# Attention and expert layer on one core: a head's five output tiles in one PSUM bank, normalised from PSUM

## The chip, the cores and the metric

The kernel runs on one core of one Trainium2 chip. The metric is device microseconds from start to end of one execution; lower is better. The engines are PE (TensorE: matmuls, with its weight loads shown as PEld), DVE (VectorE), ACT (ScalarE), POOL (GpSimd) and SP, which issues most transfers. Each engine works through a queue of its own in order. PSUM, into which PE writes its results, has eight banks of 512 float32 per partition; DVE and ACT can read it.

## The reference

An attention over 4 batches of 8 heads (1152 keys, 576 pooled queries, head size 64), followed by a mixture of 8 experts of which each token takes one.

```python
q_pool = q.reshape(B, H, S // 2, 2, D).mean(axis=3)
scores = scale * np.matmul(q_pool, k.transpose(0, 1, 3, 2))
scores = scores - np.max(scores, axis=-1, keepdims=True)
attn = np.exp(scores)
attn = attn / (np.sum(attn, axis=-1, keepdims=True) + 1e-09)
x = np.matmul(attn, v)          # heads side by side: 2304 tokens x 512
# expert layer: argmax of a cosine router, softmax gate,
# out = gate * (relu(x @ w1[e]) @ w2[e]) for the chosen expert e
```

## The kernel before

Every float32 operand of a matmul is split into a 16-bit high part and a 16-bit rest, and products are sums of two or three matmuls. The attention stage is a loop over 32 heads `g` (two heads are a pair `p`; 16 pairs). Each head has nine slots `c`, one for each chunk of 128 keys, and in each slot the code issues, in the order `ORDER = 'SMEPLX'`:

- **S** (`sc`, L274): the scores of chunk `c` for 512 of the 576 queries, two matmuls of 512 columns into a bank of `ps_s` (L268); ACT takes the exponential (L278) into `E32`.
- **M** (`mx_half`, L212): maxima for the head that comes next. Approximate row maxima come from single matmuls, without the smallest of the split products (L224, L231), written to a tile `m` of `ps_m`, which has two banks; DVE reduces the tile to one number a row (L239). Five tiles in a pair, listed in `MXA`, go another way: ACT copies the tile to a 16-bit tile `my` (L235) and DVE reduces the copy (L237), put off by `mpend` to the next slot.
- **E** (`lo_part`, L270): the rest of the exponentials, `E32` minus its high half, on POOL or DVE by the lists `POOL_EL` and `POOL_LO` (L272).
- **P** (`pv`, L329): output tiles of the head before. Four tiles of 128 queries and a fifth of 64 (the last queries). For each of nine chunks a pair of matmuls: high part by `[V high, ones, V low]`, 129 columns (L363), and rest by `[V high, ones]`, 65 columns (L364). Each tile has a bank of `ps_p` (two banks), and ACT copies it to `AC` in SBUF when it is done (L366).
- **L** (`sl`, L283): scores of the last 64 queries, 64 columns a chunk (L268, tile `lt`), in two groups with their exponentials (L292).
- **X**: side work. Among it `mx_send` (L248), which turns the maxima round with matmuls into a tile `mt` and has ACT write them as a row of the next head's queries, loads and splits for later pairs, and in slot 5 (`NPOS = 5`, the sixth) `norm(g - 2)`.

`norm` (L368) works on `AC`, on DVE alone: add a small constant to the row sums (L378), add the two halves of the output (L379), reciprocal (L380), multiply four tiles (L382) and the fifth (L384) into `XX`. From head 9 on, steps of the router run in between, with logits in banks of `ps_p`. PSUM is full: three banks `ps_s`, two `ps_m`, one `ps_l`, two `ps_p`.

After the loop the last head is normalised in two parts, the router finishes and the expert blocks run; their weights, loaded by SP and split by ACT, DVE and POOL, take the rest of the time. The order of every engine's queue is the order in which this code is written; the tile framework only adds the waits.

Of the kernel before, what the change touches and what calls it, by code (L numbers as in the profile page):

```python
# [42 lines left out]
def attn_moe(ctx: ExitStack, tc: tile.TileContext, qt, kt, vt, emb, tau, w1, w2, out):  # L43
# [35 lines left out]
    AC = [const.tile([128, 5, 130], F32, name=f"ac{i}") for i in range(2)]  # L79
# [34 lines left out]
    st2 = LD[:, 4:8, 0:2 * DM].rearrange("p s (c f) -> p s c f", c=2)  # L114

# [89 lines left out]
    mpend = []  # L205
    work_step = [0]

    def mx_flush(lag=0):
        while mpend and mpend[0][0] + lag <= work_step[0]:
            mpend.pop(0)[1]()  # L210

    def mx_half(g, t, j):  # L212
        p, h = divmod(g, 2)
        b = p // NP
        s = p % NB2
        if (p, h) not in mc:
            mc[p, h] = work.tile([128, 3, 5], F32, tag="mc", name="mc")
        m = ps_m.tile([128, 512], F32, tag="m", name="m")
        k0 = 512 * j
        w = 512 if j < 2 else S - 1024  # L220
        ts = t if j == 2 else (t,)
        for i, u in enumerate(ts):
            if u == 4:
                nc.tensor.matmul(out=m[:, i * w:(i + 1) * w], lhsT=BD[s], rhs=hn_t[p][0][:, 0, k0:k0 + w], start=True, stop=True)  # L224
            elif p < MXN:
                c = t0(b, u)
                k, q = hn_t[p]
                nc.tensor.matmul(out=m[:, i * w:(i + 1) * w], lhsT=q[64 * h:64 * h + 64, 0, c:c + 128], rhs=k[64 * h:64 * h + 64, 0, k0:k0 + w], start=True, stop=True)
            else:
                c = t0(b, u)  # L230
                nc.tensor.matmul(out=m[:, i * w:(i + 1) * w], lhsT=QQ[s][:, h, 0, c:c + 128], rhs=KK[s][:, h, 0, k0:k0 + w], start=True, stop=True)  # L231
        n = len(ts)
        if n == 1 and [ts[0], j] in (MXA[h] if g else MXAP):
            y = work.tile([128, 512], BF16, tag="my", name="my")[:, 0:w]
            nc.scalar.activation(out=y, in_=m[:, 0:w], func=AF.Copy)  # L235
            o = mc[p, h][:, j, ts[0]:ts[0] + 1]
            mpend.append((work_step[0], lambda: nc.vector.tensor_scalar(out=y, in0=y, scalar1=-3e38, scalar2=None, op0=ALU.max, op1=ALU.max, accum_out=o)))  # L237
            return
        nc.vector.tensor_reduce(out=mc[p, h][:, j, ts[0]:ts[0] + n], in_=m[:, 0:n * w].rearrange("p (t k) -> p t k", t=n), axis=AX.X, op=ALU.max)  # L239

    def mx_row(g, lo=0, hi_=5):
        p, h = divmod(g, 2)
        n = min(hi_, 5 if h == 0 else 4)
        m = mc[p, h]
        mx_flush()
        nc.vector.tensor_reduce(out=MH[g % 2][:, 64 + lo:64 + n], in_=m[:, :, lo:n].rearrange("p j t -> p t j"), axis=AX.X, op=ALU.max)

    def mx_send(g, main=True, left=True):  # L248
        p, h = divmod(g, 2)
        b = p // NP  # L250
        s = p % NB2
        c = t0(b, 0)
        if main:
            t = ps_p.tile([128, 512], F32, tag="p", name="mt")
            for i in range(4):
                nc.tensor.matmul(out=t[0:65, 128 * i:128 * i + 128], lhsT=MH[g % 2][:, i:i + 65], rhs=ident, start=True, stop=True)
            nc.scalar.activation(out=QQ[s][64:65, h, 1, c:c + 512], in_=t[64:65], func=AF.Copy, scale=-1.0, bias=ESL)
        if h == 0 and left:
            l0 = lo0(b)
            t = ps_p.tile([128, 512], F32, tag="p", name="mt")  # L260
            nc.tensor.matmul(out=t[0:65, 0:128], lhsT=MH[g % 2][:, 4:69], rhs=ident, start=True, stop=True)
            nc.scalar.activation(out=QQ[s][64:65, :, 1, l0:l0 + 64], in_=t[64:65, 0:128].rearrange("o (h q) -> o h q", h=2), func=AF.Copy, scale=-1.0, bias=ESL)
# [52 lines left out]
    MPOS = [0, 0, 0]  # L315
    NPOS = 5
# [14 lines left out]
    MXN = 2  # L331
# [18 lines left out]

    def pv(g, t, c0_, c1_):
        p, h = divmod(g, 2)
        b, i = divmod(p, NP)
        s = p % NB2
        if t < 4:
            c0, n, o = t0(b, t), 128, 0
        else:
            c0, n, o = lo0(b), 64, 64 * (b % 2)
        if c0_ == 0:
            acc[0] = ps_p.tile([128, 512], F32, tag="p", name="acc")  # L360
        a = acc[0]
# [115 lines left out]
    def front(b, c1, now=False):  # L477
# [8 lines left out]
        def logit(i, L=None):  # L486
# [3 lines left out]
            L = ps_p.tile([128, 512], F32, tag="p", name="L")  # L490
# [32 lines left out]
    def chains(b, last=None):  # L523
# [14 lines left out]
        def rank():  # L538
            L = ps_p.tile([128, 512], F32, tag="p", name="L")
# [64 lines left out]
    def place_steps():  # L604
        L = ps_p.tile([128, 512], F32, tag="p", name="L")
# [32 lines left out]
    def place_end(bs, R):  # L638
        L3 = ps_p.tile([128, 512], F32, tag="p", name="L3")
# [28 lines left out]
    def early_steps():  # L668
# [12 lines left out]
        def count():  # L681
            L = ps_p.tile([128, 512], F32, tag="p", name="L")
# [3 lines left out]
        def place():  # L686
            L = ps_p.tile([128, 512], F32, tag="p", name="L")
# [229 lines left out]
    with tc.manual_schedule():  # L917
# [55 lines left out]
        for g in range(NG + 1):  # L973
# [164 lines left out]
```

## Time and profile before

| | |
|---|---|
| time, median of 3 runs | 830.55 us (829.19 to 832.94) |
| span of the profiled execution | 825.5 us |
| busy: PE / DVE / ACT / POOL | 675.6 / 714.2 / 541.5 / 500.3 us |
| weight loads (PEld) | 377.1 us, in part under matmuls |
| start, loads and first maxima | about 0 to 45 us |
| attention heads | about 45 to 545 us |
| end of the router, expert blocks | about 545 to 825 us |

The profiled execution has no time of its own in the records besides its span. The span goes from the first to the last instruction; the median of the runs lies 5.05 us above it. The busy time of PE overstates its work, since matmuls overlap one another. A busy DVE instruction may include a time in which it stands still.

### The profile page before, as it was taken

What the parts mean: (1) busy time and instruction counts of PE and PEld (TensorE: products, weight loads), DVE (VectorE), ACT (ScalarE), POOL (GpSimd) and SP (SyncE); (2) the same over time, 40 slices, a digit from 0 to 9 for tenths busy, and PEclk for the clock granted to TensorE, in tenths of its full rate; (3) what the DMA queues carried; (4) which work ended last, traced back from release to release, by engine and by line L of the source; (5) the groups of instructions that cost most, each with busy time, mean ns of one, the idle gap of its engine ahead of it and who ended that gap; (6) DMA issues with size and microseconds to landing.
All of it is one profiled execution on the core that took longest, in us unless ns stands there. A gap on an engine that the chain in (4) does not pass through costs nothing. (4 is left out here: it accounts for less than half of the span.)

```text
span 825.5 us, 16490 instructions
## 1 busy us (share of the span) xinstructions
PE 675.6 (82%) x5963; PEld 377.1 (46%) x5963; DVE 714.2 (87%) x1121; ACT 541.5 (66%) x1077; POOL 500.3 (61%) x378
## 2 busy tenths in 40 slices
PE   8896887968969768788787887778888897999694
PEld 2353555645545445555455555533333343433241
DVE  5899989899999899999898999874165897999796
ACT  3684667767758659667685775651164767987484
POOL 4686767655657567566584654573273665766364
PEclk9698889898989899999898998888999999999998
DMA  7542342437423427614325515953999998555993
GB/s 211 176 125 62 121 119 61 125 65 193 121 67 117 119 62 196 173 35 138 84 91 142 141 28 159 161 79 80 240 307 327 321 226 220 109 123 113 193 194 78
DMA packets 124856, 117.63 MB, mean 142 GB/s; under 512 B 95214, under 2 KB 98958, under 8 KB 124768
## 3 DMA queue, kind: packets, MB, share of 16 engines
q1 hardware_dynamic: 121168, 105.48, 51.5%
q0 software_dynamic: 3600, 11.03, 4.5%
q8 instruction: 48, 0.79, 0.4%
q14 instruction: 40, 0.33, 0.1%
HBM read 116.44 MB, written 10.23 MB: 153 GB/s over the span
## 5 line engine op out<-in xcount | busy, mean ns | idle before, releaser
L272 POOL TENSOR_TENSOR ar<-ar 128x512 f16<-128x512 f32 (+1 forms) x206 | 234.2, 1144 | 176.7 <-ACT ar L278 114.2
L783 DVE TENSOR_TENSOR ar<-ld,ar 128x1024 bf16<-128x1024 f32 x100 | 174.6, 1790 | 25.2 <-ACT ar L781 24.4
L278 ACT ACTIVATE ar<-st 128x512 f32<-128x512 f32 x288 | 170.0, 596 | 33.2 <-PE st L268 31.7
L239 DVE TENSOR_REDUCE mc<-m 128x1 f32<-128x512 f32 (+2 forms) x260 | 165.1, 655 | 27.6 <-PE m L231 22.2
L363 PEld LDWEIGHTS <-ar 128*128 128x128 bf16 (+1 forms) x1440 | 145.0, 109 | 88.8 <-issue 76.4
L268 PE MATMUL st<-ar 128*128 128x512 f16 x576 | 184.7, 407 | 0.5 <-ACT ar L278 0.5
L781 ACT ACTIVATE ar<-ld 128x1024 f16<-128x1024 f32 x144 | 145.5, 1051 | 54.9 <-DMA ld<-in_w_dram 54.7
L363 PE MATMUL acc<-ar 128*128 128x129 f16 (+1 forms) x1440 | 173.8, 233 | 4.9 <-ACT ac L366 2.2
L364 PE MATMUL acc<-ar 128*128 128x65 f16 (+1 forms) x1440 | 167.2, 203 | 3.2 <-POOL ar L272 2.1
L364 PEld LDWEIGHTS <-ar 128*128 128x128 f16 (+1 forms) x1440 | 141.5, 107 | 32.8 <-issue 13.4
L231 PE MATMUL m<-ar 128*128 128x512 f16 x336 | 99.8, 347 | 62.0 <-DVE mc L239 61.3
L827 PE MATMUL ops<-ar 128*128 128x512 f16 (+1 forms) x504 | 120.9, 395 | 26.9 <-DMA ar<-ar 25.4
L272 DVE TENSOR_TENSOR ar<-ar 128x512 f16<-128x512 f32 (+1 forms) x146 | 140.4, 977 | 0.4 <-ACT ar L278 0.4
L783 POOL TENSOR_TENSOR ar<-ld,ar 128x1024 bf16<-128x1024 f32 x44 | 98.2, 2237 | 52.3 <-ACT ar L781 51.1
L799 PE MATMUL hps<-ar 128*128 128x512 f16 (+1 forms) x504 | 117.5, 388 | 6.5 <-DMA ar<-ar 5.2
L366 ACT ACTIVATE ac<-acc 128x129 f32<-128x129 f32 (+1 forms) x160 | 44.5, 278 | 104.6 <-PE acc L364 101.9
L827 PEld LDWEIGHTS <-ar 128*128 128x128 f16 x504 | 49.4, 101 | 95.7 <-DMA ar<-ar 36.1
L799 PEld LDWEIGHTS <-ar 128*128 128x128 f16 x504 | 49.4, 99 | 68.8 <-issue 7.4
L268 PEld LDWEIGHTS <-ar 128*128 128x128 f16 (+1 forms) x1152 | 63.7, 101 | 26.9 <-issue 10.1
L231 PEld LDWEIGHTS <-ar 128*128 128x128 f16 x336 | 31.8, 101 | 81.7 <-issue 54.6
L835 POOL DMA_INDIRECT out_dram<-ar,six x21 | 29.5, 1407 | 49.3 <-ACT ar L834 41.1
L806 DVE SCALAR_TENSOR_TENSOR ar<-hps,ar 128x512 f16<-128x512 f32 x38 | 25.8, 680 | 31.5 <-ACT ar L805 31.5
(273 smaller groups left out, 806.4 us busy)
## 6 DMA issues: line engine op xcount, KB each, us to landing
ld<-in_w_dram SPq DMA_DIRECT2D x156, 512.0 KB
ld<-in_q_dram SPq DMA_DIRECT2D x16, 576.0 KB
ld<-in_v_dram SPq DMA_DIRECT2D x16, 576.0 KB
ar<-ld SPq DMA_DIRECT2D x31, 288.0 KB
ld<-in_k_dram SPq DMA_DIRECT2D x15, 576.0 KB
ar<-ld SPq DMA_DIRECT2D x33, 144.0 KB
ar<-qhl SPq DMA_DIRECT2D x32, 144.0 KB
xs<-xh SPq DMA_DIRECT2D x13, 256.0 KB
```

The lines of the kernel that those rows point to most:

```text
L231: nc.tensor.matmul(out=m[:, i * w:(i + 1) * w], lhsT=QQ[s][:, h, 0, c:c + 128], rhs=KK[s][:, h, 0, k0:k0 + w], start=True, stop=True)
L239: nc.vector.tensor_reduce(out=mc[p, h][:, j, ts[0]:ts[0] + n], in_=m[:, 0:n * w].rearrange("p (t k) -> p t k", t=n), axis=AX.X, op=ALU.max)
L268: nc.tensor.matmul(out=out, lhsT=KK[s][0:n, h, k, c * 128:(c + 1) * 128], rhs=QQ[s][0:n, h, k, q0:q1], start=(k == 0), stop=(k == 1))
L272: eng.tensor_tensor(out=x(EL[g % 2]), in0=e, in1=hi(e), op=ALU.subtract)
L278: nc.scalar.activation(out=e, in_=st, func=AF.Exp, scale=1.0 / 16)
L363: nc.tensor.matmul(out=a[o:o + n, 0:129], lhsT=hi(E32[g % 2][:, c, c0:c0 + n]), rhs=VV[s][:, h, c, 0:129], start=(c == 0), stop=False)
L364: nc.tensor.matmul(out=a[o:o + n, 0:65], lhsT=EL[g % 2][:, c, c0:c0 + n], rhs=VV[s][:, h, c, 0:65], start=False, stop=(c == NC - 1))
L366: nc.scalar.activation(out=AC[g % 2][o:o + n, t, 0:129], in_=a[o:o + n, 0:129], func=AF.Copy)
L781: nc.scalar.activation(out=dh, in_=src, func=AF.Copy)
L783: eng.tensor_tensor(out=dl.bitcast(BF16), in0=src, in1=dh, op=ALU.subtract)
L799: nc.tensor.matmul(out=hp[j, f], lhsT=xt[:, 2 * c + i // 2], rhs=wv(w, i % 2, c)[:, f * 512:(f + 1) * 512], start=(k == 0), stop=(k == 11))
L827: nc.tensor.matmul(out=op[j], lhsT=ht[:, c + 4 * (c // 4) + 4 * (i // 2)], rhs=wv(w, i % 2, c), start=(k == 0), stop=(k == 23))
```

## The change

`pv` keeps all five tiles of a head in one bank of `ps_p`, 65 columns a tile, and for each chunk issues three matmuls instead of two: the low half of V is added onto the same 64 columns. The fifth tile is computed 128 rows wide for eight of its nine chunks. The copies to `AC` are gone, and `norm` reads the bank itself, without the add of the halves; its slot stays the sixth. All tiles of the maxima are reduced by DVE from PSUM. Since two heads now hold the two banks of `ps_p`, `mt` and the router's small tiles go to `ps_m` while the loop runs (`small`).

```diff
@@ mx_half @@
-        if n == 1 and [ts[0], j] in (MXA[h] if g else MXAP):
-            y = work.tile([128, 512], BF16, tag="my", name="my")[:, 0:w]
-            nc.scalar.activation(out=y, in_=m[:, 0:w], func=AF.Copy)
-            o = mc[p, h][:, j, ts[0]:ts[0] + 1]
-            mpend.append((work_step[0], lambda: nc.vector.tensor_scalar(out=y, in0=y, scalar1=-3e38, scalar2=None, op0=ALU.max, op1=ALU.max, accum_out=o)))
-            return
         nc.vector.tensor_reduce(out=mc[p, h][:, j, ts[0]:ts[0] + n], in_=m[:, 0:n * w]..., axis=AX.X, op=ALU.max)
@@ mx_send @@
-            t = ps_p.tile([128, 512], F32, tag="p", name="mt")
+            t = ps_m.tile([128, 512], F32, tag="m", name="mt")
@@ router @@
+    def small(name):
+        if ended:
+            return ps_p.tile([128, 512], F32, tag="p", name=name)
+        return ps_m.tile([128, 512], F32, tag="m", name=name)
-            L = ps_p.tile([128, 512], F32, tag="p", name="L")
+            L = small("L")
@@ pv @@
-        if c0_ == 0:
-            acc[0] = ps_p.tile([128, 512], F32, tag="p", name="acc")
-        a = acc[0]
-            nc.tensor.matmul(out=a[o:o + n, 0:129], lhsT=hi(E32[g % 2][:, c, c0:c0 + n]), rhs=VV[s][:, h, c, 0:129], start=(c == 0), stop=False)
-            nc.tensor.matmul(out=a[o:o + n, 0:65], lhsT=EL[g % 2][:, c, c0:c0 + n], rhs=VV[s][:, h, c, 0:65], start=False, stop=(c == NC - 1))
-        if c1_ == NC:
-            nc.scalar.activation(out=AC[g % 2][o:o + n, t, 0:129], in_=a[o:o + n, 0:129], func=AF.Copy)
+        if t == 0 and c0_ == 0:
+            acc[g] = ps_p.tile([128, 512], F32, tag="p", name="acc")
+        a = acc[g][:, 65 * t:65 * t + 65]
+            nc.tensor.matmul(out=a[r], lhsT=hi(e[:, w]), rhs=VV[s][:, h, c, 0:65], start=(x == 0), stop=False)
+            nc.tensor.matmul(out=a[r, 0:64], lhsT=hi(e[:, w]), rhs=VV[s][:, h, c, 65:129], start=False, stop=False)
+            nc.tensor.matmul(out=a[r], lhsT=el[:, w], rhs=VV[s][:, h, c, 0:65], start=False, stop=(x == NC - 1))
@@ norm @@
-        a = AC[g % 2]
+        a = acc[g][:, 0:325].rearrange("p (t k) -> p t k", k=65)
         nc.vector.tensor_scalar(out=r[ps, ts], in0=a[ps, ts, 64:65], scalar1=VS * ES * 1e-9, scalar2=None, op0=ALU.add)
-        nc.vector.tensor_tensor(out=xs_[ps, ts], in0=a[ps, ts, 0:64], in1=a[ps, ts, 65:129], op=ALU.add)
         nc.vector.reciprocal(out=r[ps, ts], in_=r[ps, ts])
-            nc.vector.tensor_tensor(out=X[b % 2][:, :, hc], in0=xs_[:, 0:4], in1=r[:, 0:4].to_broadcast([128, 4, 64]), op=ALU.mult)
+            nc.vector.tensor_tensor(out=X[b % 2][:, :, hc], in0=a[:, 0:4, 0:64], in1=r[:, 0:4].to_broadcast([128, 4, 64]), op=ALU.mult)
-            nc.vector.tensor_scalar(out=XX[o:o + 64, 4, hc], in0=xs_[o:o + 64, 4], scalar1=r[o:o + 64, 4], ...)
+            nc.vector.tensor_scalar(out=XX[o:o + 64, 4, hc], in0=a[o:o + 64, 4, 0:64], scalar1=r[o:o + 64, 4], ...)
```

On DVE, the normalisation in an odd head and what follows it. Before:

```order
L272 TENSOR_TENSOR ar<-ar 128x512
L378 TENSOR_SCALAR r<-ac_81 128x5
L379 TENSOR_TENSOR xs__1555<-ac_81 128x320
L380 RECIPROCAL r<-r 128x5
L382 TENSOR_TENSOR xx<-xs__1555,r 128x4x64
L384 TENSOR_SCALAR xx<-xs__1555,r 64x64
L239 TENSOR_REDUCE mc<-m 128x1
L237 TENSOR_SCALAR my,mc<-my 128x512
L239 TENSOR_REDUCE mc<-m 128x1
```

The same place with the change (the line numbers are those of the changed code: L267 is L272 of before, L235 is L239):

```order
L267 TENSOR_TENSOR ar<-ar 128x512
L378 TENSOR_SCALAR r<-acc 128x5
L379 RECIPROCAL r<-r 128x5
L381 TENSOR_TENSOR xx<-acc,r 128x4x64
L383 TENSOR_SCALAR xx<-acc,r 64x64
L235 TENSOR_REDUCE mc<-m 128x1 x3
```

The add is gone, the other four read the bank `acc`, and the three maxima behind them all read `m`.

On PE, two chunks of an output tile (`ar` holds the exponentials and V). Before:

```order
L363 LDWEIGHTS ar
L363 MATMUL acc<-ar 128x129
L364 LDWEIGHTS ar
L364 MATMUL acc<-ar 128x65
L363 LDWEIGHTS ar
L363 MATMUL acc<-ar 128x129
L364 LDWEIGHTS ar
L364 MATMUL acc<-ar 128x65
```

One chunk of it with the change:

```order
L365 LDWEIGHTS ar
L365 MATMUL acc<-ar 128x65
L366 LDWEIGHTS ar
L366 MATMUL acc<-ar 128x64
L367 LDWEIGHTS ar
L367 MATMUL acc<-ar 128x65
```

The columns of a chunk stay 194; the weights of the high part are loaded twice.

On ACT, the second half of an odd head (L160 and L166 split the next keys and queries). Before:

```order
L366 ACTIVATE ac_80<-acc 128x129
L278 ACTIVATE ar<-st 128x512
L235 ACTIVATE my<-m 128x512
L366 ACTIVATE ac_80<-acc 128x129
L160 ACTIVATE ld<-ld 128x288
L278 ACTIVATE ar<-st 128x512
L257 ACTIVATE ar<-mt 1x512
L262 ACTIVATE ar<-mt 1x2x64
L278 ACTIVATE ar<-st 128x512
L366 ACTIVATE ac_80<-acc 64x129
L292 ACTIVATE ar<-lt 128x5x64
```

The same stretch with the change:

```order
L273 ACTIVATE ar<-st 128x512 x2
L166 ACTIVATE ld<-ld 128x288
L273 ACTIVATE ar<-st 128x512
L252 ACTIVATE ar<-mt 1x512
L257 ACTIVATE ar<-mt 1x2x64
L273 ACTIVATE ar<-st 128x512
L287 ACTIVATE ar<-lt 128x5x64
```

The copies to `ac` and `my` are gone from between the exponentials; `mt` stands where it stood, in a bank of `ps_m`.

## Rows read from the trace of the kernel before

**Rows 1.** Table of stages: busy us PE, PEld, DVE, ACT, POOL; clock; DMA; GB/s.

```profile
141.70:173.00 31.30, 25.57 (x288) 16.47 (x288) 29.04 (x50) 21.48 (x51) 20.53 (x18) 0.89 0.36 100
45.00:520.00 475.00, 384.42 (x4446) 249.53 (x4445) 447.73 (x830) 326.09 (x770) 303.55 (x255) 0.91 0.42 111
```

**Rows 2.** Waits of DVE, PE, 45 to 520 us: total, times, longest.

```profile
DVE mc L239 <- PE m L231: 22.2, 25, 1.4
PE m L231 <- DVE mc L239: 61.3, 55, 3.6
PE m L224 <- DVE mc L239: 16.0, 12, 2.1
```

**Rows 3.** Timeline, DVE then POOL, inside one normalisation: start, length, instruction.

```profile
124.98 1.05 DVE L382 TENSOR_TENSOR xx<-xs__1803,r 128x256 f32<-128x256 f32 x1
125.95 1.08 DVE L384 TENSOR_SCALAR xx<-xs__1803,r 64x64 f32<-64x64 f32 x1
...
124.51 1.24 POOL L272 TENSOR_TENSOR ar<-ar 128x512 f16<-128x512 f32 x1 [0.42 <-ACT ar L278]
125.94 1.04 POOL L272 TENSOR_TENSOR ar<-ar 128x512 f16<-128x512 f32 x1 [0.19 <-ACT ar L278]
```

**Rows 4.** Stage table of L378, L379, L380, L382, L384 alone: DVE busy (instructions).

```profile
45.00:520.00 475.00, 19.50 (x30) 0.91 0.42 111
45.00:520.00 475.00, 15.18 (x30) 0.91 0.42 111
45.00:520.00 475.00, 5.29 (x30) 0.91 0.42 111
45.00:520.00 475.00, 29.84 (x30) 0.91 0.42 111
45.00:520.00 475.00, 16.58 (x30) 0.91 0.42 111
```

**Rows 5.** Durations min/median/max of two DVE lines that read PSUM.

```profile
L492 DVE COPY lraw<-L x13: 146/152/167, 192.8 to 469.3; 128x8 f32<-128x8 f32 x13
L806 DVE SCALAR_TENSOR_TENSOR ar<-hps,ar x38: 676/678/692, 585.1 to 807.7; 128x512 f16<-128x512 f32 x38
```

**Rows 6.** Groups of DVE instructions, 45 to 520 us: count, busy, mean ns.

```profile
L272 DVE TENSOR_TENSOR ar<-ar 128x512 f16<-128x512 f32 x89 | 89.1, 1001 | 0.0
```

**Rows 7.** DVE timeline, maxima one after the other.

```profile
133.16 0.67 DVE L237 TENSOR_SCALAR_CACHE_REDUCE my<-my 128x512 bf16<-128x512 bf16 x1
133.77 0.68 DVE L239 TENSOR_REDUCE mc<-m 128x1 f32<-128x512 f32 x1
134.37 0.67 DVE L237 TENSOR_SCALAR_CACHE_REDUCE my<-my 128x512 bf16<-128x512 bf16 x1
```

**Rows 8.** Groups of ACT over the span: count, busy, mean ns, idle before.

```profile
L235 ACT ACTIVATE my<-m 128x512 bf16<-128x512 f32 x76 | 45.1, 594 | 9.3 <-PE m L231 6.6 <-PE m L228 2.6
L366 ACT ACTIVATE ac<-acc 128x129 f32<-128x129 f32 (+1 forms) x160 | 44.5, 278 | 104.6 <-PE acc L364 101.9
```

**Rows 9.** PE timeline: output tiles, score columns, one wait for a bank.

```profile
125.37 0.22 PE L363 MATMUL acc<-ar 128*128 128x129 f16 x1
125.43 0.19 PE L364 MATMUL acc<-ar 128*128 128x65 f16 x1
125.46 0.22 PE L363 MATMUL acc<-ar 128*128 128x129 f16 x1
...
136.10 0.35 PE L268 MATMUL lt<-ar 128*128 128x64 f16 x6
136.30 0.60 PE L268 MATMUL st<-ar 128*128 128x512 f16 x2
...
144.16 0.58 PE L231 MATMUL m<-ar 128*128 128x512 f16 x1 [3.40 <-DVE mc L239]
```

**Rows 10.** DVE timeline after the last head.

```profile
539.66 1.90 DVE L378 TENSOR_SCALAR r<-ac 128x4 f32<-128x4 f32 x1
...
542.00 2.15 DVE L382 TENSOR_TENSOR xx<-xs__8488,r 128x256 f32<-128x256 f32 x1
```

More of the change, by code (lines that the diff above doesn't have):

```diff
@@ L114, in attn_moe @@
     st2 = LD[:, 4:8, 0:2 * DM].rearrange("p s (c f) -> p s c f", c=2)
+    ended = []
+    def small(name):
+        if ended:
+            return ps_p.tile([128, 512], F32, tag="p", name=name)
+        return ps_m.tile([128, 512], F32, tag="m", name=name)
     raw = {}
@@ L204, in attn_moe @@
     mc = {}
[L205 to L210, printed above, removed]
     def mx_half(g, t, j):
@@ L222, in mx_half @@
         for i, u in enumerate(ts):
+            k, q = hn_t[p]
+            both = u == 4 or p < MXN
+            kr = (k[:, 0] if both else KK[s][:, h, 0])[:, k0:k0 + w]
+            o = m[:, i * w:(i + 1) * w]
             if u == 4:
[L224 to L228, printed above, removed]
+                nc.tensor.matmul(out=o, lhsT=BD[s], rhs=kr, start=True, stop=True)
             else:
                 c = t0(b, u)
[L231 removed]
+                r = slice(64 * h, 64 * h + 64) if both else slice(0, 128)
+                qr = q[r, 0] if both else QQ[s][r, h, 0]
+                nc.tensor.matmul(out=o, lhsT=qr[:, c:c + 128], rhs=kr[r], start=True, stop=True)
         n = len(ts)
[L233 to L238 removed]
         nc.vector.tensor_reduce(out=mc[p, h][:, j, ts[0]:ts[0] + n], in_=m[:, 0:n * w].rearrange("p (t k) -> p t k", t=n), axis=AX.X, op=ALU.max)
@@ L259, in mx_send @@
             l0 = lo0(b)
-            t = ps_p.tile([128, 512], F32, tag="p", name="mt")
+            t = ps_m.tile([128, 512], F32, tag="m", name="mt")
             nc.tensor.matmul(out=t[0:65, 0:128], lhsT=MH[g % 2][:, 4:69], rhs=ident, start=True, stop=True)
@@ L315, in attn_moe @@
     MPOS = [0, 0, 0]
+    MXN = 2
     NPOS = 5
@@ L349, in attn_moe @@
     acc = {}
+    E32F = [view(i * SET, F32, NC * SQ) for i in range(2)]
+    ELF = [view(i * SET + 4 * NC * SQ, F16, NC * SQ) for i in range(2)]
     def pv(g, t, c0_, c1_):
@@ L538, in rank @@
         def rank():
-            L = ps_p.tile([128, 512], F32, tag="p", name="L")
+            L = small("L")
             nc.tensor.matmul(out=L[:, 0:n * NE], lhsT=tri, rhs=o.rearrange(F), start=True, stop=False)
@@ L604, in place_steps @@
     def place_steps():
-        L = ps_p.tile([128, 512], F32, tag="p", name="L")
+        L = small("L")
         T0, n, _ = tiles(B - 1)
@@ L619, in base @@
         def base():
-            L2 = ps_p.tile([128, 512], F32, tag="p", name="L2")
+            L2 = small("L2")
             nc.tensor.matmul(out=L2[:, 0:16], lhsT=nbh, rhs=tri8, start=True, stop=True)
@@ L638, in place_end @@
     def place_end(bs, R):
-        L3 = ps_p.tile([128, 512], F32, tag="p", name="L3")
+        L3 = small("L3")
         for T in range(NT):
@@ L681, in count @@
         def count():
-            L = ps_p.tile([128, 512], F32, tag="p", name="L")
+            L = small("L")
             nc.tensor.matmul(out=L[:, 0:NE], lhsT=ones, rhs=rsp[:, B - 1], start=True, stop=True)
@@ L686, in place @@
         def place():
-            L = ps_p.tile([128, 512], F32, tag="p", name="L")
+            L = small("L")
             for T in range(LT):
@@ L1070, in attn_moe @@
                         f()
+        ended.append(True)
         cut, rest, squares, logit = last_part(B - 1)
```

33 lines of the change are left out of this document (13 added, 20 removed).

## The prediction

> **What bounds the kernel now.** I read the table of stages first. From 45 to 520 us, thirty heads, DVE is busy 447.7 of 475 us, 94%; PE 384.4, ACT 326.1, POOL 303.6 [rows 1]. The clean pair 141.7 to 173.0 says the same: DVE 29.0 of 31.3 us, PE 25.6 [rows 1]. Next the waits, to see who waits for whom: in those 475 us PE waits 61.3 + 16.0 = 77.3 us for DVE to give back a bank of maxima, and DVE waits 22.2 us for PE's matmuls of maxima [rows 2]. So DVE's queue sets the pace and PE stands behind it. What is taken out of DVE's queue shortens a head; what is taken off ACT alone does not.
>
> Third, the timeline of one normalisation, DVE beside POOL. L382 runs from 124.98 to 126.03 and POOL's instruction of 124.51 ends at 125.75; the next DVE instruction, L384, begins at 125.95 beside a POOL instruction of 125.94 and ends at 127.03, POOL's at 126.98 [rows 3]. L384 handles 64 numbers a row, and L382 256; both take over 1 us. So these instructions stand still until POOL's current one has ended. Per normalisation the five lines take 0.65 + 0.51 + 0.18 + 0.99 + 0.55 = 2.88 us, 86.4 us for thirty [rows 4].
>
> **The change, part by part.**
>
> *Normalisation.* The add (0.51 us) goes. The three that read SBUF and wait now read PSUM. Two lines of the trace read PSUM on DVE and are nearly constant, although POOL works beside many of them: a copy of 8 numbers takes 146 to 167 ns (median 152), an instruction with one PSUM and one SBUF input of 512 numbers 676 to 692 (678) [rows 5]. Between them a number costs (678 - 152) / 504 = 1.04 ns. My estimates are then 0.15 us for the constant, 0.152 + 248 x 1.04 = 0.41 for the four tiles, 0.152 + 56 x 1.04 = 0.21 for the fifth; the reciprocal keeps its 5.29 / 30 = 0.18 [rows 4]. Together 0.95 instead of 2.88 us: 1.93 x 30 = **-58 us**. The other end: the waits stay and only the add goes, 15.2 us [rows 4]. I take the first end, since L806 has the same kinds of operands as the new multiplication.
>
> [...]
>
> *Last heads.* Outside 45 to 520 lie two more normalisations. After the last head L378 takes 1.90 us and L382 2.15 [rows 10]; at 0.15 and 0.41 they would give back 3.5 us, on the way to the last tokens' routing. Part of this returns as the next DVE instruction's wait for POOL. I take **-3**, bounds 0 and -4.
>
> *Maxima.* L237 on the 16-bit copy starts at 133.16, the reduction from PSUM at 133.77, the next L237 at 134.37 [rows 7]: 0.61 against 0.60 us. Five a pair change from one to the other, 76 in all: nothing on DVE, 0 from both sides within 1 us.
>
> *ACT.* 45.1 us of copies to `my` and 44.5 us of copies of output tiles go, with 104.6 us in which ACT waited in its queue for output tiles [rows 8]. ACT is not what DVE waits for [rows 2], so I count nothing. It has one side effect: ACT used to give a maxima bank back in 0.59 us; now DVE does it when its queue comes to it. That is in the ring below.
>
> *PE.* A pair of matmuls, 129 and 65 columns, takes 125.37 to 125.46, some 88 ns over a run of them; the 65 column one 30 of these, its own weight load included [rows 9]. The three new ones have 65, 64 and 65 columns. Six 64-column matmuls, each with its load, take 136.10 to 136.30, 33 ns each [rows 9]. So a chunk costs 90 to 100 instead of 88 ns; 45 chunks a head, 32 heads, 1440 chunks: +3 to +17 us of PE, I say 9. The cover is the 77.3 us in which PE waits for DVE [rows 2]; without it those 9 us would be added. The fifth tile's 128 rows instead of 64 cost nothing there, since time goes by columns.
>
> *POOL.* DVE's other instructions still wait for POOL. The rests of the exponentials on DVE take 1001 ns in the mean for 512 numbers, 89 of them [rows 6], against 678 for a size that does not wait [rows 5]: 0.32 x 89 = 29 us of waiting. With POOL's 303.6 us in 420 instead of 475, its share rises from 64 to 72%, and the waits with it: **+4 us**, bounds 0 and +10.
>
> *The ring of maxima banks.* `ps_m` now also carries `mt` and the router's tiles. In an odd head the order on PE is two maxima tiles, one more, `mt`, a second `mt`, the scores of slot 8, two maxima tiles. The second `mt` must wait until DVE has reduced the tile two before it; before, only the later maxima did. Behind it in PE's queue stand the scores of slot 8, and ACT and POOL wait for these. But PE already stands for DVE in this place: 3.40 us at 144.16, just after a normalisation [rows 9], and that wait shrinks by about the 1.9 us that the normalisation gets shorter. While PE does `mt`, 0.4 us, scores 0.5 and maxima, DVE has a rest of the exponentials of 0.7 to 1.3 us to do. So DVE idles little: 0 to 1 us a pair, +0 to +15 us, I take **+4**. Against it stands DVE's idle time of today, 475 - 447.7 = 27 us, part of it behind that long stall, where the clock granted to PE falls (0.89 over the pair [rows 1]); a shorter stall may give back up to 20 us, I take **-4**.
>
> **Sum.** -58 - 3 + 0 + 0 + 4 + 4 - 4 = -57 us, from 825.5 to 768.5 us of span. The median of the runs is 5.05 us above the span, so I forecast 830.55 - 57 = **773.5 us**. What is late next is still DVE: 447.7 - 58 + 4 = 394 of 418 us, with PE at 393 close behind it.
>
> **The rivals.**
>
> *The ring eats half.* DVE starves once a head because PE waits for `mt`'s copy or for DVE itself: one PE chain of a `mt` and scores, about 1 us, in each of 32 heads: +32 us on the forecast, 805. For it: two banks for all, PE and DVE nearly equal after the change. Against it: today's waits are of PE for DVE, three to one [rows 2].
>
> *A larger gain.* PE, never stalled for long, keeps the full clock, and DVE's 27 us of idle time go: 773.5 - 25 = 748. For it: the stall of 3.40 us is the longest kind [rows 2] and is cut by half.
>
> *The waits stay.* DVE reading PSUM still waits for POOL, since it writes SBUF and takes `r` from it. Only the add goes: 830.55 - 15 = 815. Against it: 38 instructions of L806 between 676 and 692 ns [rows 5].
>
> *PE becomes the bound, slower.* If a matmul can't follow another with a fresh load in less than the 57 ns that the 129-column one takes now (88 - 30 [rows 9]), a chunk takes 171 ns: +83 x 1440 = 120 us of PE, 112 of it in the stage. PE's 384 become 496 us [rows 1], over the 475 of today, and the time is about 830.55 + 21 + 5 for the ring = 856. It decides from 88 + 33 / 1350 us, some 112 ns a chunk, where PE passes DVE, and turns into a loss at about 155 ns. Against it are the 30 and 33 ns rows [rows 9].
>
> [...]
>
> **How the numbers follow.** Forecast 0.62; ring 0.13; larger gain 0.12; waits stay 0.05; PE bound 0.08. A difference of 0.5%, 4 us, is about what a measurement of this kernel can tell from no change. All cases but the last are faster; of the ring's 0.13 I put 0.03 at a loss of the whole gain, within 0.5%. Faster 0.89, same 0.03, slower 0.08. For the range, the upper end takes in the ring at 805, the lower end the larger gain at 748; the slow case, the worse part of the ring and the waits that stay are left out: 748 to 806.
>
> **What would show it.** Right: the multiplication of the four tiles at 0.40 to 0.45 us with POOL busy beside it, the normalisation under 1.1 us, a clean pair of 27 to 28 us, the pace of a chunk 88 to 100 ns, PE's waits for maxima banks below 60 us in the stage. Wrong: normalisations over 2 us (waits stay); DVE's idle time in the stage over 50 us with waits for maxima matmuls behind `mt` (ring); chunks over 112 ns and DVE under 85% busy (PE). A change in the expert blocks, which the edit leaves alone apart from their start, would also break the sum.

## The result and the profile after

The changed kernel takes **783.0 us** (median of 4 runs, 777.5 to 784.2) against 829.9 us of the kernel before on the same chip (828.0 to 832.9): ratio 0.942, interval 0.938 to 0.946. The prediction was 773.5 us with a range of 748 to 806. The sign and the range held; 47 us were gained where 57 were forecast. The profiled execution has a span of 781.4 against 825.5 us.

The page's first part, of the changed kernel (engine, busy us, share of the span, instructions):

```profile
PE 665.6 (85%) x7403; PEld 380.1 (49%) x7403; DVE 652.1 (83%) x1010; ACT 469.9 (60%) x841; POOL 488.3 (62%) x378
```

Next the table of stages (window, its length, busy us and instructions of PE, PEld, DVE, ACT and POOL, granted clock, share of the DMA engines, GB/s). I cut it at the reciprocals of the first and the thirtieth normalisation, since the same work, 29 heads, lies between these in both kernels. The kernel before:

```profile
57.64:518.95 461.31, 370.73 (x4284) 241.43 (x4282) 434.15 (x807) 315.54 (x743) 294.16 (x240) 0.91 0.41 109
```

The changed kernel, the same stretch, and one clean pair of heads, which is one without steps of the router:

```profile
63.16:474.01 410.85, 357.42 (x5550) 242.19 (x5547) 379.93 (x706) 250.04 (x531) 285.24 (x240) 0.95 0.46 122
108.93:134.32 25.39, 22.66 (x354) 15.19 (x351) 24.09 (x42) 15.92 (x34) 20.19 (x18) 1.00 0.44 124
```

The 44.1 us of span divide so: the first normalisation comes 63.2 - 57.6 = 5.5 us later; the 29 heads between take 410.9 instead of 461.3, 50.5 us less; from the thirtieth to the last normalisation 22.8 instead of 27.9, 5.1 less; from there to the end 284.6 instead of 278.6, 6.0 more. DVE is still what sets the pace: its work fell by 434.2 - 379.9 = 54.2 us, and its idle time in the stretch rose from 27.2 to 30.9. A clean pair went from 31.3 us [rows 1] to 25.4.

The groups of DVE, 45 to 520 us, of the changed kernel (line, operation, shapes and count; busy us, mean ns of one; idle before). L378 to L383 are the normalisation, L267 the rests of the exponentials, L235 the maxima:

```profile
L235 DVE TENSOR_REDUCE mc<-m 128x1 f32<-128x512 f32 x260 | 170.5, 681 | 26.5 <-PE m L233 20.6 <-PE m L228 5.3
L267 DVE TENSOR_TENSOR ar<-ar 128x512 f16<-128x512 f32 x94 | 82.7, 881 | 0.2
L381 DVE TENSOR_TENSOR xx<-acc,r 128x256 f32<-128x256 f32 x32 | 13.6, 425 | 1.1
L383 DVE TENSOR_SCALAR xx<-acc,r 64x64 f32<-64x64 f32 x32 | 8.9, 279 | 0.3
L379 DVE RECIPROCAL r<-r 128x5 f32<-128x5 f32 x31 | 5.9, 191 | 1.1
L378 DVE TENSOR_SCALAR r<-acc 128x5 f32<-128x5 f32 x31 | 4.7, 150 | 0.0
```

The four lines add to 0.150 + 0.191 + 0.425 + 0.279 = 1.05 us, where five took 2.88 [rows 4]. The timeline of one of them (start, length, instruction) stands against [rows 3]:

```profile
173.41 0.15 DVE L378 TENSOR_SCALAR r<-acc 128x5 f32<-128x5 f32 x1
173.59 0.19 DVE L379 RECIPROCAL r<-r 128x5 f32<-128x5 f32 x1
173.82 0.42 DVE L381 TENSOR_TENSOR xx<-acc,r 128x256 f32<-128x256 f32 x1
174.26 0.29 DVE L383 TENSOR_SCALAR xx<-acc,r 64x64 f32<-64x64 f32 x1
```

and POOL's row of the same moment:

```profile
172.44 2.52 POOL L267 TENSOR_TENSOR ar<-ar 128x512 f16<-128x512 f32 x2 [0.44 <-ACT ar L273]
```

POOL works from 172.44 to 174.96, through the whole normalisation, and nothing of DVE stands still for it. The multiplication took 425 ns with `acc` in PSUM against 1.05 us with `xs_` in SBUF [rows 3], and in the means the constant went from 0.65 us [rows 4] to 0.150 and the fifth tile from 0.55 [rows 4] to 0.279. Why the source in PSUM takes the wait away, these rows do not show.

The waits of PE, then of DVE, in the stretch of the changed kernel (engine, line, what it waited for: total us, times, longest):

```profile
PE m L233 <- DVE mc L235: 14.8, 26, 2.4
PE m L228 <- DVE mc L235: 12.8, 13, 2.0
PE m L228 <- DVE lraw L491: 6.9, 3, 2.6
PE L L470 <- DVE mc L235: 5.9, 9, 1.5
PE mt L256 <- DVE mc L235: 3.9, 13, 0.5
...
DVE mc L235 <- PE m L233: 20.1, 45, 1.4
```

Against [rows 2] PE's waits for maxima banks fell from 77.3 to 27.6 us. Three kinds are new, and all come from `ps_m` being shared: maxima that wait for the router's copy (L491), router logits that wait for maxima (L470), and transposed maxima that wait for maxima (L256).

Last the pace of a chunk, PE's timeline inside one output tile:

```profile
121.44 0.19 PE L367 MATMUL acc<-ar 128*128 128x65 f16 x1
121.47 0.19 PE L365 MATMUL acc<-ar 128*128 128x65 f16 x1
121.50 0.19 PE L366 MATMUL acc<-ar 128*128 128x64 f16 x1
121.53 0.19 PE L367 MATMUL acc<-ar 128*128 128x65 f16 x1
...
122.18 0.19 PE L367 MATMUL acc<-ar 128*128 128x65 f16 x1
```

From 121.44 to 122.18 are eight chunks, 92.5 ns each, 88 before [rows 9]. A single load lasts 99 to 101 ns in the means of L365 to L367 in the profile of the changed kernel, and yet a chunk with three of them takes 92.5: the loads overlap one another and the matmuls.

### The profile page after: what moved, and what is told of

It is laid out like the page before. It is cut to its first block, busy times and chain, and to the rows that moved or that the text cites. A ratio compares the mean times of both kernels' runs of the same rounds, so it can differ in the third digit from the quotient of the medians.

```text
span 781.4 us, 19108 instructions
## 1 busy us (share of the span) xinstructions
PE 665.6 (85%) x7403; PEld 380.1 (49%) x7403; DVE 652.1 (83%) x1010; ACT 469.9 (60%) x841; POOL 488.3 (62%) x378
## 5 line engine op out<-in xcount | busy, mean ns | idle before, releaser
L267 POOL TENSOR_TENSOR ar<-ar 128x512 f16<-128x512 f32 (+1 forms) x206 | 232.2, 1137 | 135.4 <-ACT ar L273 125.7
L235 DVE TENSOR_REDUCE mc<-m 128x1 f32<-128x512 f32 x336 | 213.2, 662 | 37.3 <-PE m L233 29.6
L782 DVE TENSOR_TENSOR ar<-ld,ar 128x1024 bf16<-128x1024 f32 x100 | 169.7, 1739 | 31.0 <-ACT ar L780 30.4
L263 PE MATMUL st<-ar 128*128 128x512 f16 x576 | 182.6, 402 | 2.3 <-ACT ar L273 2.0
L367 PE MATMUL acc<-ar 128*128 128x65 f16 (+1 forms) x1440 | 168.7, 195 | 4.2 <-DVE ar L267 2.5
L365 PE MATMUL acc<-ar 128*128 128x65 f16 (+1 forms) x1440 | 169.2, 197 | 0.0
L366 PE MATMUL acc<-ar 128*128 128x64 f16 (+1 forms) x1440 | 168.5, 198 | 0.0
L365 PEld LDWEIGHTS <-ar 128*128 128x128 bf16 (+1 forms) x1440 | 138.7, 99 | 60.3 <-issue 40.9
L366 PEld LDWEIGHTS <-ar 128*128 128x128 bf16 (+1 forms) x1440 | 138.8, 100 | 25.0 <-issue 4.4
L367 PEld LDWEIGHTS <-ar 128*128 128x128 f16 (+1 forms) x1440 | 138.9, 101 | 5.0 <-DVE ar L267 2.7
L267 DVE TENSOR_TENSOR ar<-ar 128x512 f16<-128x512 f32 (+1 forms) x146 | 127.9, 891 | 1.4 <-ACT ar L273 1.3
L233 PE MATMUL m<-ar 128*128 128x512 f16 x336 | 90.3, 333 | 15.1 <-DVE mc L235 14.8
L826 PEld LDWEIGHTS <-ar 128*128 128x128 f16 x504 | 48.9, 100 | 99.8 <-DMA ar<-ar 40.8
L798 PEld LDWEIGHTS <-ar 128*128 128x128 f16 x504 | 49.9, 100 | 69.7 <-issue 8.6
L263 PEld LDWEIGHTS <-ar 128*128 128x128 f16 (+1 forms) x1152 | 63.8, 100 | 40.6 <-issue 29.3
```

The lines of the kernel that those rows point to most:

```text
L233: nc.tensor.matmul(out=o, lhsT=qr[:, c:c + 128], rhs=kr[r], start=True, stop=True)
L263: nc.tensor.matmul(out=out, lhsT=KK[s][0:n, h, k, c * 128:(c + 1) * 128], rhs=QQ[s][0:n, h, k, q0:q1], start=(k == 0), stop=(k == 1))
L267: eng.tensor_tensor(out=x(EL[g % 2]), in0=e, in1=hi(e), op=ALU.subtract)
L365: nc.tensor.matmul(out=a[r], lhsT=hi(e[:, w]), rhs=VV[s][:, h, c, 0:65], start=(x == 0), stop=False)
L366: nc.tensor.matmul(out=a[r, 0:64], lhsT=hi(e[:, w]), rhs=VV[s][:, h, c, 65:129], start=False, stop=False)
L367: nc.tensor.matmul(out=a[r], lhsT=el[:, w], rhs=VV[s][:, h, c, 0:65], start=False, stop=(x == NC - 1))
```

## The experiments

My theory after this result: the normalisation gives its 55 to 60 us because it no longer waits for POOL, and the missing 10 us went into the shared ring of maxima banks. The rivals: it is the missing add and the missing queue for ACT that count, or the third matmul or the maxima eat the difference. Each part was undone in the changed kernel or put alone into the kernel before. All were timed in three rounds beside the kernel before, whose median in the three sessions was 828.6, 829.2 and 830.5 us.

### Is it the wait for POOL?

**norm_sbuf**: the changed kernel, but ACT copies the bank to SBUF in one instruction and DVE reads the copy. No add comes back.

```diff
+        if t == 4 and c1_ == NC:
+            nc.scalar.activation(out=AC[g % 2], in_=acc[g][:, 0:325], func=AF.Copy)
...
-        a = acc[g][:, 0:325].rearrange("p (t k) -> p t k", k=65)
+        a = AC[g % 2].rearrange("p (t k) -> p t k", k=65)
```

> The changed kernel, but ACT copies a finished head's whole bank (325 numbers a row) to SBUF in one instruction and the normalisation reads that copy; no add, no other copies, maxima from PSUM as in the change. Theory 'POOL': the saving is that the normalisation's operands left SBUF, so that it no longer waits for POOL. Then its constant, multiplication and fifth-tile instructions go back to means of 0.65, 0.99 and 0.55 us, a normalisation takes about 2.4 instead of 1.0 us, and 32 heads lose 40 to 45 us: 823 to 828 us. Rival 'add and ACT': the saving came from the removed add and from ACT's 160 copies; then 783 to 790 us, with a normalisation of about 1 us.

Measured: 843.5 us (839.3 to 850.8), ratio 1.018 [1.011, 1.025]. The same four lines of DVE, from its first to its thirtieth normalisation:

```profile
L384 DVE TENSOR_TENSOR xx<-ac,r 128x256 f32<-128x256 f32 x29 | 27.2, 937 | 1.0
L386 DVE TENSOR_SCALAR xx<-ac,r 64x64 f32<-64x64 f32 x29 | 22.1, 761 | 0.2
L381 DVE TENSOR_SCALAR r<-ac 128x5 f32<-128x5 f32 x29 | 20.1, 693 | 0.0
L382 DVE RECIPROCAL r<-r 128x5 f32<-128x5 f32 x30 | 5.7, 191 | 1.0
```

Same work, other source: 937 for 425 ns, 761 for 279, 693 for 150; the reciprocal, which reads SBUF in both, keeps its 191. That the difference is a wait for POOL, and not a dearer read, the same trace shows. A multiplication that met POOL at work, POOL's row of that moment, and one that found POOL idle:

```profile
109.62 1.23 DVE L384 TENSOR_TENSOR xx<-ac,r 128x256 f32<-128x256 f32 x1
109.30 1.27 POOL L176 TENSOR_TENSOR qhl<-qs,qhl 128x576 f16<-128x576 f32 x1
...
530.87 0.42 DVE L384 TENSOR_TENSOR xx<-ac,r 128x256 f32<-128x256 f32 x1
```

POOL's instruction ends at 110.57, and the multiplication 0.28 us later. The five multiplications beside which POOL ran nothing take 424 to 426 ns, as from PSUM, and the fourteen such instructions of the fifth tile 237 to 255. So PSUM as the source is what takes the wait away. The copy itself is hardly waited for: DVE stood for it once, 2.1 us. The whole gain is gone, and the time is 15 us above the kernel before. The loss, 60 us, is above the 32 x 1.54 = 49 us by which the lines grew, and above what I expected.

**norm_sbuf_s**: the same edit in the kernel with the ring undone (mt_router_s, below), to see whether the 60 us came through the ring.

> The normalisation from an SBUF copy, as in the run of that name, but with mt and the router's tiles in the scores' banks. If the waits for POOL alone cost: 1.4 us in 32 heads, 43 us over 760.6: 800 to 806 us. If the part over 43 us (843.5 against 783.0, 60 us) belongs to the waits and not to the shared banks: 815 to 822.

Measured: 820.4 us (816.7 to 822.2), ratio 0.989 [0.986, 0.993], 59.8 us over mt_router_s. So the 60 us belong to the normalisation's source and not to the ring. Its stretch from the first to the thirtieth normalisation:

```profile
58.87:507.77 448.90, 369.09 (x5566) 247.91 (x5564) 419.93 (x705) 257.27 (x560) 291.20 (x239) 0.93 0.43 112
```

and that of mt_router_s:

```profile
58.13:449.00 390.87, 344.86 (x5533) 235.51 (x5530) 378.17 (x705) 248.53 (x530) 290.00 (x239) 0.98 0.49 128
```

DVE's work differs by 41.8 us, its idle time by 29.0 - 12.7 = 16.3, and the clock by 0.93 against 0.98. I read this as a chain, which no run takes apart: a DVE that is later makes PE wait, the clock granted to PE is then lower, and DVE in turn waits longer for PE.

### What does the ring of maxima banks cost?

**ring_m**: the kernel before, with `mt` and the router's tiles in `ps_m` and nothing else changed.

```diff
-            t = ps_p.tile([128, 512], F32, tag="p", name="mt")
+            t = ps_m.tile([128, 512], F32, tag="m", name="mt")
...
-            L = ps_p.tile([128, 512], F32, tag="p", name="L")
+            L = small("L")
```

> The kernel before, with the turned maxima and the router's small tiles in the two banks of the maxima: the bank sharing of the change alone. By the prediction's term (+4, bounds 0 and 15): 830 to 845 us. By the run that took these tiles out of the changed kernel's maxima banks (760.6 against 783): +20 or more, 848 to 860, since DVE's stalls are longer here.

Measured: 843.8 us (840.0 to 848.1), ratio 1.018 [1.014, 1.023], 14.7 us slower. The waits of PE from its first to its thirtieth normalisation, and of DVE:

```profile
PE m L238 <- DVE mc L246: 29.0, 36, 3.2
PE mt L263 <- DVE mc L246: 27.2, 10, 3.7
PE m L231 <- DVE mc L246: 11.1, 10, 2.1
PE mt L268 <- DVE mc L246: 10.9, 13, 1.9
...
DVE mc L246 <- PE m L238: 34.3, 44, 1.7
```

`mt` now waits 38.1 us for DVE. PE's total for these four is 78.2 us, about the 77.3 of [rows 2]: this wait did not grow, it moved to an earlier place in PE's queue, ahead of `mt` and of the scores behind it. What grew is DVE's wait for PE, from 22.2 [rows 2] to 34.3 us: 12 of the 14.7. As a side effect PE's maxima also wait 12.6 us for the router's copy.

**mt_only_s, router_s_again, mt_router_s**: the changed kernel with `mt` alone, the router's tiles alone, or both in the score banks `ps_s`.

```diff
-        return ps_m.tile([128, 512], F32, tag="m", name=name)
+        return ps_s.tile([128, 512], F32, tag="s", name=name)
...
-            t = ps_m.tile([128, 512], F32, tag="m", name="mt")
+            t = ps_s.tile([128, 512], F32, tag="s", name="mt")
```

> As the one with the router's tiles in the scores' banks, and the turned maxima (mt) there as well. Theory 'ring': the wait of 2.2 us for a bank at 34.2 in the second head and the low clock after it go too, the first normalisation comes at 58 to 59 instead of 63 us, and the time falls by 10 to 15 us against the change, to 768 to 773. Rival: mt in the scores' banks delays the scores instead, and the time is that of the run with the router's tiles alone, or more.

> The changed kernel with the transposed maxima alone in the score banks; the router's small tiles stay in the maxima banks. With both out the time fell from 783.0 to 760.6 us. If the transposed maxima, two in an odd head and one in an even head, are what the ring costs: 760 to 768 us and the clean pairs unchanged near 25 us, the router's heads still 18 us. If the router's tiles cost it: 775 to 782 us, with the first normalisation near 63 us moving to 58 either way, since only the transposed maxima run there.

> The changed kernel with the router's small tiles alone in the score banks, run beside the two others. If the two parts of the ring add up, this and the run with the transposed maxima alone divide the 22 us between them: 768 to 776 us where the router's heads fall from 18.5 to 16.5 us (four of them in the stage, 8 us), or 780 to 784 where those heads' gain is lost again at the start, where the first normalisation is then still at 63 us.

Measured: both, **760.6 us** (756.2 to 761.6), ratio 0.917 [0.914, 0.920], the fastest of all; `mt` alone 768.1 (760.3 to 771.0), 0.923 [0.917, 0.929]; the router alone 780.8 (773.2 to 782.3), 0.938 [0.933, 0.944]. The ring costs the changed kernel 22 us, 15 of them by `mt`; the router's tiles alone give 2, which is no difference that these runs can tell, though its heads fell from 18.3 to 16.3 us; with `mt` out already, taking them out gives 7.5. The router's edit was run once before, as router_s, at 781.2 us with a spread of 767.5 to 786.4, too wide to use:

> The changed kernel, with the router's small tiles in the loop in the three banks of the scores instead of the two of the maxima. Theory 'ring': in three stretches of router work PE waits for a maxima bank that holds logits (2.6 us at 183.5 in the changed kernel, then a lower clock); a head of 18.3 us goes to 16 or less and the time falls by 6 to 10 us, to 773 to 777. Rival: these heads are long because DVE has the router's own work (17.4 us before the change too): 781 to 785 us.

Part of `mt`'s 15 us may lie at the start. PE's timeline of the changed kernel shows `mt` of the second head behind a reduction of DVE, and later the maxima behind the router's copy:

```profile
31.20 0.63 PE L233 MATMUL m<-ld,qhl 64*128 64x512 f16 x1
...
34.22 0.58 PE L251 MATMUL mt<-ident,mh 128*65 128x128 f16 x4 [2.17 <-DVE mc L235]
...
183.52 0.58 PE L228 MATMUL m<-ld,bd 128*128 128x512 f16 x1 [2.56 <-DVE lraw L491]
```

The clock granted around them, in the table of stages of the changed kernel:

```profile
40.00:50.00 10.00, 10.00 (x125) 5.89 (x125) 8.11 (x13) 5.76 (x12) 5.99 (x6) 0.69 0.03 9
...
184.00:190.00 6.00, 6.00 (x74) 4.07 (x73) 3.46 (x7) 3.50 (x9) 2.73 (x2) 0.54 0.38 94
```

and of mt_router_s, the first window, with the same L233 that stands ahead of that `mt`:

```profile
28.60 0.63 PE L233 MATMUL m<-ld,qhl 64*128 64x512 f16 x1
...
40.00:50.00 10.00, 10.00 (x156) 5.82 (x155) 9.41 (x15) 7.07 (x16) 7.98 (x7) 0.98 0.21 49
```

PE is full in both, but it does 125 instructions at 0.69 and 156 at 0.98. From 30 to 40 us, in which the first stall lies, the clock is 0.50 in both kernels, and in mt_router_s it comes back earlier, 0.98 against 0.69 from 40 to 50 us. The first normalisation is at 63.2 us in the changed kernel, 58.1 in mt_router_s, and 61.2 with `mt` alone taken out. But these 5 us are not shown to be the price of the stall and the clock: the L233 before it already comes 2.6 us earlier in mt_router_s, norm_sbuf, which has the same stall of 2.2 us, has its first normalisation at 60.3, and ring_m has it at 57.5, as the kernel before. The second stall is followed by six microseconds with a clock of 0.54.

### What did the copies of maxima on ACT cost?

**max_dve**: the kernel before, with all maxima read from PSUM (`MXA` empty). **max_act**: the changed kernel with the five copies of a pair back, reduced on DVE in 16 bits as before.

```diff
-    MXA = [[[1, 1], [3, 1], [3, 0], [1, 0]], [[0, 0]]]
+    MXA = [[], []]
```

max_act, without the lines that keep the list of deferred reductions:

```diff
+        if n == 1 and [ts[0], j] in (MXA[h] if g else []):
+            y = work.tile([128, 512], BF16, tag="my", name="my")[:, 0:w]
+            nc.scalar.activation(out=y, in_=m[:, 0:w], func=AF.Copy)
...
+            mpend.append((work_step[0], lambda: nc.vector.tensor_scalar(out=y, in0=y, scalar1=-3e38, scalar2=None, op0=ALU.max, op1=ALU.max, accum_out=o2)))
+            return
```

> The kernel before, with all maxima reduced by DVE from PSUM (no 16-bit copies by ACT): this part of the change alone. By the prediction's term (0 on DVE): 826 to 834 us. Rival, from the run with the copies put back into the changed kernel (807 against 783 us): the copies cost 20 us or more in themselves, and the time falls to 805 to 812.

> The changed kernel with the five maxima tiles of a pair through ACT's 16-bit copy again, as before the change. Theory 'POOL': DVE's time is the same either way (0.61 against 0.60 us a tile), and ACT gives five banks a pair back earlier: 778 to 785 us. Rival 'ACT': ACT's freed 45 us are a part of the gain, and the time goes to 795 or more.

Measured: max_dve 824.2 us (817.0 to 826.8), ratio 0.993 [0.988, 0.999], 5 us faster, which is only just clear of the noise; max_act 807.5 (803.1 to 810.8), 0.974 [0.968, 0.980], 24.5 us slower than the changed kernel, which I had not expected. I then thought that the ring made it dear, and tested that.

**best1**: mt_router_s with the same copies.

> The kernel with the transposed maxima and the router's small tiles in the score banks (760.6 us), and the five maxima of a pair go back to the copy on ACT and the 16-bit reduction on DVE. The same step cost 24 us (807.5 against 783.0) where these tiles shared the two maxima banks. Theory that the shared banks made it dear (a bank given back late also holds up the transposed maxima): with the tiles elsewhere the copies cost no more than the 5 us that they cost in the kernel before, 756 to 768 us, clean pairs of 25 to 26 us. Rival, the copies and the deferred reductions are dear by themselves once DVE is 97% busy: 778 us or more, clean pairs of 28 us or more.

Measured: 784.8 us (779.0 to 788.3), ratio 0.947 [0.944, 0.950]: 24 us again, with clean pairs of about 28 us. That theory falls; the ring has no part in it. The rows of DVE show where it lies. best1, 60 to 450 us (L280 are the rests, L245 the 16-bit maxima):

```profile
L280 DVE TENSOR_TENSOR ar<-ar 128x512 f16<-128x512 f32 x81 | 81.7, 1009 | 0.0
L245 DVE TENSOR_SCALAR_CACHE_REDUCE my<-my 128x512 bf16<-128x512 bf16 x68 | 45.7, 672 | 0.3
L280 DVE TENSOR_TENSOR ar<-ar 128x320 f16<-128x320 f32 x14 | 23.3, 1664 | 0.0
L280 DVE TENSOR_TENSOR ar<-ar 128x256 f16<-128x256 f32 x27 | 21.0, 776 | 0.0
```

mt_router_s, the same window:

```profile
L267 DVE TENSOR_TENSOR ar<-ar 128x512 f16<-128x512 f32 x85 | 75.7, 891 | 0.2
L267 DVE TENSOR_TENSOR ar<-ar 128x320 f16<-128x320 f32 x15 | 20.6, 1372 | 0.0
L267 DVE TENSOR_TENSOR ar<-ar 128x256 f16<-128x256 f32 x28 | 16.9, 605 | 0.0
```

The 16-bit reduction itself is no dearer, 672 against 679 ns. But the rests, which wait for POOL (in the changed kernel those of 512 numbers beside which POOL ran nothing take 668 to 693 ns, and those over 720 end 541 to 553 ns after an instruction of POOL has ended), take 118 to 292 ns more each: 81 x 118 + 14 x 292 + 27 x 171 ns = 18.3 us. From the first to the thirtieth normalisation best1 takes 413.5 us, 22.6 more than mt_router_s: 15.9 of DVE's work and 6.8 of its idle time. POOL is not slower for it, 1153 against 1184 ns for its own rests of 512; and about as many of DVE's rests wait, 40 of 81 against 43 of 85 take over 720 ns, but these take 1348 ns in the mean against 1097. The pair of max_dve and the kernel before shows the same, 847 against 1001 ns [rows 6]. max_dve, 45 to 520 us:

```profile
L272 DVE TENSOR_TENSOR ar<-ar 128x512 f16<-128x512 f32 x89 | 75.4, 847 | 0.2
L196 DVE SCALAR_TENSOR_TENSOR ar<-ld,ar 128x576 f16<-128x576 f32 x30 | 32.4, 1082 | 0.1
```

There the rests give back 89 x 154 ns = 13.7 us, 19.6 with their two smaller sizes; the split of V, L196, takes 8.0 more (24.4 us in the kernel before) and the normalisation, which waits for POOL there, 4.2 more, so little is left. Why rests wait less for POOL when the maxima beside them come from PSUM was not settled. Whether the deferral, by which the 16-bit reductions stand later in DVE's queue, has a part in it was not tried.

### What does the third matmul cost?

**third_mm**: the kernel before, its 129-column matmul cut into 65 and 64 columns.

```diff
-            nc.tensor.matmul(out=a[o:o + n, 0:129], lhsT=hi(E32[g % 2][:, c, c0:c0 + n]), rhs=VV[s][:, h, c, 0:129], start=(c == 0), stop=False)
+            nc.tensor.matmul(out=a[o:o + n, 0:65], lhsT=hi(E32[g % 2][:, c, c0:c0 + n]), rhs=VV[s][:, h, c, 0:65], start=(c == 0), stop=False)
+            nc.tensor.matmul(out=a[o:o + n, 65:129], lhsT=hi(E32[g % 2][:, c, c0:c0 + n]), rhs=VV[s][:, h, c, 65:129], start=False, stop=False)
```

> The kernel before, with the high part's matmul of 129 columns cut in two, of 65 and 64 columns, each with its own load of the weights: the change's third matmul alone. Theory 'cover': a chunk takes 90 to 96 ns instead of 88, and PE's waits for DVE take up the 3 to 12 us: 828 to 834 us. Rival 'PE': the second load shows, a chunk goes over 110 ns and the time to 840 or more.

Measured: 836.0 us (834.0 to 837.4), ratio 1.008 [1.005, 1.012], 6.8 us slower. Waits of PE, 45 to 520 us, of third_mm:

```profile
PE m L231 <- DVE mc L239: 57.2, 50, 3.5
PE m L224 <- DVE mc L239: 13.3, 11, 2.1
PE mt L261 <- DVE lraw L493: 7.1, 3, 2.9
```

PE's waits for maxima banks shrank from 77.3 to 70.5 us, as a cover would, and yet the time rose. A second wait grew: L261, 3.0 us in the kernel before, takes 7.1. In the two profiled executions the span differs by 8.2 us, 4.7 of it between the first and the thirtieth normalisation and 2.2 before the first. I read this as PE work that was in part not in the places where PE stands; no run takes it apart.

## Why the prediction was right, and where its sum was off

**What bounds the kernel.** Right: DVE before and after, and 54 us less DVE work gave 50 us less time in the same stretch.

**Normalisation, forecast -58.** Right in mechanism and size: 1.83 us less each, 55 us in thirty, by durations, and 60 by both runs that put the SBUF source back. The two are not the same quantity: those runs leave the add out, 0.51 us a head, and no run has the add alone. The estimate from L806 gave 0.41 for the four tiles, 0.425 measured; the fifth tile took 0.28 where I took 0.21, so the line that I drew through two other kinds of instruction was too cheap for it. Where POOL was idle, norm_sbuf's multiplication took 424 to 426 ns from SBUF against 425 from PSUM, and only the fifth tile is dearer from PSUM, 279 against 237 to 255; in the kernel before, the two took 424 to 427 and 238 to 255 from SBUF where POOL was idle.

**Last heads, forecast -3.** Measured -5.1 from the thirtieth to the last normalisation, a stretch that also holds the last heads' other work. The two instructions by themselves give 3.5: no L378 of the changed kernel takes over 0.17 us and no L381 over 0.43.

**Maxima, forecast 0 "from both sides within 1 us".** This step failed. I compared the two forms' own pace, 0.61 and 0.60 us [rows 7], which was right, and did not ask what they do to the rests of the exponentials beside them, which take 118 ns more each beside the 16-bit form. Worth 5 us in the kernel before, 24 us in the changed one.

**PE's third matmul, forecast 0 behind a cover of 77 us.** The pace was right, 92.5 ns for 90 to 100. The cover was not whole: 6.8 us in the kernel before. A total of waits over a stage does not say that the waits lie where the added work lies.

**POOL, forecast +4.** Wrong sign: the rests fell from 1001 [rows 6] to 881 ns, 94 x 0.12 = 11 us less. With the copies of the maxima back (max_act) they take 1036, so it is the same effect as that of the maxima, not one more.

**Ring, forecast +4 of 0 to +15.** The place and the mechanism were right (the second `mt`, the scores behind it), and the size was off: 14.7 us in the kernel before, 22 in the changed one, the end of the bounds or beyond. I argued that PE stands for DVE in this place already, so that only a shift follows. ring_m shows just that shift, 78 us of waits as before, and it costs all the same: DVE's waits rise by 12 us, which my 0 to 1 us a pair allowed for at its upper end only. The start of the program, outside the stage that I read, was left out: the first normalisation comes 5 us later than in mt_router_s, and 2.6 of these lie before the stall.

**Clock and idle, forecast -4.** The clock rose from 0.91 to 0.95 in the stretch, to 0.98 without the ring; DVE's idle time stayed (27.2 and 30.9). What the clock gave was not measured apart.

**Expert blocks, forecast no change.** 6.0 us longer after the last normalisation. In the other kernels this part takes 278.3 to 284.7 us, 278.3 in mt_router_s; what sets it was not found.

**The sum.** Parts measured alone, in us: normalisation -60 (its source, without the add), third matmul +7, maxima -5 (in the kernel before) or -24 (in the changed one), ring +15 or +22. With the first values the sum is -43, with the second -55; measured is -47. The parts are not independent, and don't add to the last microsecond. Against the forecast the ring is dearer by 11 or 18 us and the third matmul by 7; the maxima are cheaper by 5 or 24 and POOL's term of 4 falls away. The expert part adds 6 to the first values; the ring's 22 hold such a difference already, 284.6 against 278.3 in mt_router_s. That makes the total 15 us worse with the first values and 3 better with the second, and 10 were missing. So part of the closeness of 773.5 to 783.0 is errors of opposite sign.

**The rivals.** Of the marks that I named, the multiplication (425 ns), the normalisation (1.05 us), the chunk (92.5 ns) and PE's waits (44.3 us in the rows above, under 60) came as forecast; a clean pair is shorter than I said, 25.4 for 27 to 28 us. "The waits stay" and "PE becomes the bound" are refuted by 1.05 us and by 92.5 ns. "The ring eats half" had the right mechanism at two thirds of its price (22 of 32 us), and was hidden by the maxima; its mark, over 50 us of DVE's idle time, did not come (30.9). "A larger gain" is what mt_router_s reaches, by a move of tiles that the change does not make: the clock at 0.98, DVE busy 378 of 391 us, and 760.6; PE's longest wait for a maxima bank is 2.4 us in the changed kernel already, where it was 3.6 [rows 2].

## What to carry to other kernels

Where DVE sets the pace beside a busy POOL, look for short DVE instructions whose operands all come from SBUF: here three lines that waited for POOL (norm_sbuf) no longer did when taken from PSUM, 150 ns for 693, 425 for 937 and 279 for 761, and the 543 ns that the constant lost for 5 numbers a row are out of proportion to its size. The reciprocal, from SBUF in both, took 191 ns in both. A small tile that stands ahead of the main chain in an engine's queue should not share a ring of banks with tiles that another, fully busy engine gives back; here the move of `mt` and the router's tiles to other banks was worth 22 us. And hidden work should be checked against where the waits lie, not against their total.

## What the runs showed of the hardware

A DVE instruction of 5 numbers a row took 150 ns from PSUM and 693 ns in the mean from SBUF beside POOL. Undoing that for three lines a head cost 60 us, of which the lines' own time is 49. The 16-bit maxima from SBUF kept their own 672 ns, yet beside them the two-input rests took 1009 ns in the mean, against 891 where the maxima came from PSUM. Three matmuls of 64 or 65 columns, each with a 128-column load of its own, follow each other at 31 ns. Behind a stall of 2.6 us PE was busy without a gap from 184 to 190 us, and the granted clock was 0.54.
